# A fused linear attention and ELU feed-forward kernel: the order of the first block's end and the steps in which block 1's units begin

## The chip, the cores and the metric

The kernel runs on one core of one Trainium2 chip. The metric is the device time of one execution in microseconds (us), shown as the median of several runs; the profile is of one further execution. A core has five engines that each work through a queue of their own in order: PE (TensorE, matmuls, with its weight loads shown as PEld), DVE (VectorE), ACT (ScalarE), POOL (GpSimd) and SP (SyncE, which here only issues DMAs). They wait for each other on semaphores.

## The reference

Four batches of 768 tokens with 8 heads of 48 columns go through a linear attention with a decaying state. The result is one row of 384 columns for each of the 3072 tokens, and a two-layer ELU network is applied to it.

```
# attention, for every batch and head
for t in range(S):
    cur = einsum('bhd,bhe->bhde', u * k[t], v[t])
    y[t] = einsum('bhd,bhde->bhe', r[t], state + cur)
    state = w * state + einsum('bhd,bhe->bhde', k[t], v[t])
# x: (3072, 384), w_in: (384, 2048), w_out: (2048, 384)
h = x @ w_in
g = where(h > 0, h, exp(minimum(h, 0)) - 1)
out = g @ w_out
```

## The kernel before

**Blocks, units and slices.** The sequence is cut into 6 blocks of 128 tokens. A block holds 128 tokens of each of the 4 batches; the attention of one batch in one block is a *unit* (n, b). A block's 512 tokens then go through the network in 16 *slices* of 128 hidden columns: the first layer of a slice (`hidden`, L1004, nine matmuls), its ELU, and the second layer (`project`, L1048, nine matmuls). The run is 6 x 16 *steps* (n, f), one slice each. PE takes its large matmuls in pieces of high and low words (`xh`, `xl`, `wh`, `wl`, `gh`, `gl`), so that every layer of a slice has three times three matmuls.

**A unit** turns its r and k by PE (`T`, L606), scales them by powers of the decay (`dr`, `dk`, L666, DVE), multiplies r and k into score matrices (`A`, L740), takes them through a mask (`pa`, `pb`, L821; in block 0 `m0`, `m1`, L666), multiplies with v (`Y`, L779 to L796), and adds to the state (`S` or the end of `Y`, L897, from `krd`, keys scaled on DVE at L712). `ru` and `sum` (L697 to L705) make the token's own term, which ACT and POOL spread into a matrix (`Eq` L810, `Dp` L814). `xh` and `xl` split the result into words.

**A slice's ELU** is a chain over two engines: ACT `neg` (L1013 relu, L1014 exp), DVE `elu` (L1019), ACT `gh` (L1025), DVE `gl` (L1027). **A slice's weights** arrive by DMA (`Lw`, `Lq`) and are split beforehand: ACT `wd` (widen, L549), DVE `ma` (merge, L558), ACT and POOL `sp` (L571, L569), DVE and POOL `r4d`, `r3` (L595, L593).

**The order is written by hand**, and every engine's queue follows it. `START` lists the operations up to the first step: it computes block 0's four units and the first slices' weights. A token is a name and a unit or slice: `Y:3` is the output of unit (0, 3), `S:0` the new state of unit (0, 0), `H:0` the first layer of slice 0 for units 0 and 1 only (256 of 512 columns), `jk:2` two small matmuls that only keep PE busy, `flip` a matmul that makes the table `rev` which `krd` reads, `Ln:1` the loads of unit (1, 1). `ZERO` lists step (0, 0), `FIRST` the other steps of block 0, `LATER` all steps after. In `FIRST` a digit behind a name is a stage of block 1's units, which run inside block 0's steps: unit (1, b) begins in step `BEGIN[b]`, has T and dr/dk in this step (stage 0), A, pa, pb and krd one step later (stage 1), Y two steps later (stage 2) and its new state three steps later (stage 3). `project` of a slice stands one step behind its `hidden`, from step 6 on two steps behind, so step 6 has no `project`.

**PSUM.** Outside the first units, the small results of PE take three banks in turn (tag `rw`): a turned r or k, a score matrix or an added state may be written only when the one three places before in the same bank has been read.

Of the kernel before, what the change touches and what calls it, by code (L numbers as in the profile page):

```python
# [20 lines left out]
B, H, S, D = 4, 8, 768, 48  # L21
# [19 lines left out]
START = """  # L41
Lrk:2 Lv:1 Lrk:3 Lv:2 Lw:0 Lw:2 Lv:3 Lw:1 Lw:4 Lw:3 Lw:5
ub Tr:0 inv ru:0 Tk:0 PT dr:0 dk:0 zw ru:1 Tr:1 dr:1 sum:0 Tk:1 vd:0 A:0 dk:1 ru:2 Tr:2 m0:0 m1:0 Tk:2 A:1 dr:2 dk:2
sum:1 sum:2 vd:1 vd:2 jk:1 Y:0 xh:0 m0:1 m1:1 Tr:3 Tk:3 A:2 xl:0 ru:3 dr:3 dk:3 m0a:2 jk:1 Y:1 m1:2 wd:0 A:3 xh:1 flip
ma:0 sp:0 sum:3 xl:1 wdi:1 rsd:0 Lw:6 vd:3 Y:2 H:0 mai:1 krd:0 spi:1 xh:2 m0:3 m1:3 rsd:2 xl:2 S:0 Ln:0 wdo:1 jk:2 Y:3
H:1 xh:3 xl:3 mao:1 spo:1 krd:1 S:1 Ln:1 wd:2 krd:2 krd:3 rsd:1
"""
ZERO = "Lq hid T0 df0 neg elu gh ma gl rud0 sum0 sp Dp0 r4d r3 wd"
FIRST = """
Lq rk3 v3 Eq1 hid S ns3 A1 T0 rud0 ma sum0 bkA-1 neg df0 elu sp dk0 pa1 brA-1 Y2 gh gl dr0 pb1 r4d xh2 xl2 mbT+1 mrT+1  # L50
proj krd1 swd2 Dp0 r3 rudx rudA-2 sumA-1 wd third tT+0
"""
LATER = """
hid AY tT+0 bkA-1 proj neg elu brA-1 pbA+2 gh gl st nsY+0 xhY+0 xlY+0 paA+1 EqA+1 krA+1 mbT+0 mrT+0 rudA-2
swA+2 sumA-1 rkY+0 vY+0 DpA+0 out
"""
BEGIN = [0, 4, 8, 11]
SCORES = [16, 20, 23, 26] + [13 + 4 * j for j in range(4, 16)]
OUTPUTS = SCORES[1:] + [77]
TURNS = [12] + SCORES[:-1]  # L60
# [3 lines left out]
class Kernel:  # L64
# [307 lines left out]
    def next_loads(self, b):  # L372
        self.raw[1, b] = self.slots[b]
        self.load_rk(1, b)
        self.load_v(1, b)

    def stages(self, n, f):
        return [(f - t, 1, b) for b, t in enumerate(BEGIN) if n == 0 and -1 <= f - t < 4]

    def units_at(self, times, step):  # L380
        return [divmod(2 * B + j, B) for j, t in enumerate(times) if t == step]
# [12 lines left out]
    def step(self, n, f):  # L394
        nc = self.nc

        k = f + 2 if n == 0 else NF + 1
        units = self.stages(n, f)


        last = divmod(n * NF + f - (1 if (n, f) < EARLY else 2), NF)
        both = {
            "ru": lambda n, b: self.current(n, b),
            "kr": lambda n, b: self.key_rest(n, b),
            "A": lambda n, b: self.scores(n, b),
            "sw": lambda n, b: self.decay_state(n, b),
            "rk": lambda n, b: self.load_after(n, b, self.load_rk),
            "ns": lambda n, b: self.new_state(n, b),
            "v": lambda n, b: self.load_after(n, b, self.load_v),
            "sum": lambda n, b: self.current_sum(n, b),  # L410
            "Dp": lambda n, b: self.diag_scores(n, b, 0),
            "Dq": lambda n, b: self.diag_scores(n, b, 1),
            "Ep": lambda n, b: self.diag_scores(n, b, 0, True),
            "Eq": lambda n, b: self.diag_scores(n, b, 1, True),
            "rud": lambda n, b: self.current(n, b, nc.vector),
            "krd": lambda n, b: self.key_rest(n, b, nc.vector),
            "swd": lambda n, b: self.decay_state(n, b, nc.vector),
            "pa": lambda n, b: self.take_scores(n, b, 0),
            "pb": lambda n, b: self.take_scores(n, b, 1),
            "Y": lambda n, b: self.outputs(n, b),  # L420
            "xh": lambda n, b: self.split_x(n, b, 0),
            "xl": lambda n, b: self.split_x(n, b, 1),
        }
        by_pe = {
            "T": lambda n, b: self.turn_in(n, b),
            "dk": lambda n, b: self.decay_k(n, b) if b else None,
            "dr": lambda n, b: self.decay_r(n, b) if b else None,
            "df": lambda n, b: self.decay_in(n, b) if b == 0 else None,
        }
        moved = {  # L430
            "t": lambda n, b: self.turn_blocks(n, b),
            "mb": lambda n, b: self.move_blocks(n, b),
            "mr": lambda n, b: self.gather_blocks(n, b),
            "br": lambda n, b: self.decay_moved(n, b, 0),
            "bk": lambda n, b: self.decay_moved(n, b, 1),
        }
        layer = {
            "hid": lambda: self.hidden(n, f, self.rest_of(n, f)),
            "ma": lambda: self.merge(k),
            "neg": lambda: self.negative(n, f),  # L440
            "sp": lambda: self.split_w(k),
            "r4": lambda: self.rest_w(k, 1),
            "r3": lambda: self.rest_w(k, 0),
            "r4d": lambda: self.rest_w(k, 1, nc.vector),
            "r3d": lambda: self.rest_w(k, 0, nc.vector),
            "elu": lambda: self.elu(n, f),
            "gh": lambda: self.split_g(n, f, 0),
            "gl": lambda: self.split_g(n, f, 1),
            "proj": lambda: self.project(*last) if last in self.g else None,
            "Lq": lambda: [self.load_weights(j) for j in (2 * k + 3, 2 * k + 4)],  # L450
            "wd": lambda: self.widen(k + 1),
            "st": lambda: self.store(last[0]) if last[1] == NF - 1 and last[0] in self.acc else None,
            "out": lambda: self.store_next(),
            "S": lambda: [self.new_state(0, b) for b in (2, 3)] if (n, f) == (0, 1) else None,
            "third": lambda: self.third_slot() if (n, f) == (0, 14) else None,
            "AY": lambda: self.insertion(now),
        }
        now = n * NF + f
        for op in (LATER if n else FIRST if f else ZERO).split():
            if op in layer:  # L460
                layer[op]()
                continue
            if op[-2] in "+-":
                name, times = op[:-3], {"A": SCORES, "Y": OUTPUTS, "T": TURNS}[op[-3]]
                for m, b in self.units_at(times, now - int(op[-2:])):
                    if (name, m, b) not in self.done:
                        self.done.add((name, m, b))
                        {**both, **moved}[name](m, b)
                continue
            name, stage = op[:-1], -1 if op[-1] == "x" else int(op[-1])  # L470
            for at, m, b in units:
                todo = {**both, **by_pe}
                if at == stage and name in todo and (name, m, b) not in self.done:
                    self.done.add((name, m, b))
                    todo[name](m, b)
# [655 lines left out]
```

## Time and profile before

| | |
|---|---|
| median of 3 runs | 511.44 us (510.69 to 511.98) |
| the profiled execution | 509.62 us, of which the span of the trace is 507.9 us |
| PE busy | 493.0 us, 97% of the span |
| DVE, ACT, POOL busy | 304.1, 242.5, 109.6 us |

The span runs from the first to the last instruction of the trace; the profiled execution took 1.7 us more than it. A busy share is the time in which an engine had an instruction running; what an engine costs is read from the waits, since the time of an engine that nobody waits for costs nothing.

### The profile page before, as it was taken

The numbers are of one execution on the slowest core, as the hardware profiler recorded it, in microseconds if no ns is written. First come the engines' busy times: TensorE is split into PE (matmuls) and PEld (weight loads), VectorE is DVE, ScalarE is ACT, GpSimd is POOL, SyncE is SP. The second block draws the span as 40 slices with busy tenths as digits, with TensorE's granted clock in tenths as the row PEclk, the third lists the DMA queues.
The fourth block names the chain that finished last, engine by engine and source line by source line (L and its number), as shares of the span: only waits on it lengthen the run. The fifth ranks groups of instructions, "written<-read, shape, count | busy, mean of one in ns | idle before, by whom it ended". The sixth has DMA issues, their size and how long they took to land.

```text
span 507.9 us, 12144 instructions
## 1 busy us (share of the span) xinstructions
PE 493.0 (97%) x5024; PEld 406.1 (80%) x5024; DVE 304.1 (60%) x528; ACT 242.5 (48%) x462; POOL 109.6 (22%) x145
## 2 busy tenths in 40 slices
PE   7969999999999999999999999999999999999995
PEld 6857887887788888888888888888888878899995
DVE  7786888885865576575574675574664443343331
ACT  2366767744444445435444354354354354344442
POOL 8514334332033141321311212211011000000000
PEclk9998999999999999999999999999999999999999
DMA  8996777765166444625623536316243000011001
GB/s 139 240 184 158 176 187 191 148 130 130 39 140 147 105 71 88 147 66 108 131 49 88 124 59 134 108 36 127 67 96 101 19 0 1 8 27 25 6 0 67
DMA packets 108453, 49.11 MB, mean 97 GB/s; under 512 B 89442, under 2 KB 104292, under 8 KB 108388
## 3 DMA queue, kind: packets, MB, share of 16 engines
q1 hardware_dynamic: 96292, 43.52, 38.5%
q10 hardware_dynamic: 12096, 4.72, 3.9%
q8 instruction: 41, 0.67, 0.6%
q14 instruction: 24, 0.20, 0.1%
HBM read 35.12 MB, written 13.11 MB: 95 GB/s over the span
## 4 chain that ended last, share of the span: by engine, by line
PE 91%; DVE 2%; DMA 2%; ACT 2%; POOL 1%; issue 1%; SPq 0%; DVEq 0%; ACTq 0%
PE ps_acc L1048 40%; PE ps_h L1004 37%; PE ps_y L796 4%; PE ps_a L764 3%; PE ps_a L740 2%; PE ps_y L784 1%; PE ps_y L897 1%; PE ps_y L779 1%; DMA k_t<-in_k_dram 1%; DMA stage<-in_moe_w_in_dram 1%; ACT wide L549 1%; PE ps_y L853 1%; POOL ru L697 0%; PE ps_kT L606 0%; DMA w_col<-in_w_dram 0%
## 5 line engine op out<-in xcount | busy, mean ns | idle before, releaser
L1004 PE MATMUL ps_h<-x,wh 128*128 128x512 f32 (+1 forms) x588 | 180.8, 389 | 0.0
L1048 PE MATMUL ps_acc<-g,wh 128*128 128x512 f32 x480 | 166.3, 401 | 0.0
L1019 DVE SCALAR_TENSOR_TENSOR ps_h<-g,ps_h 128x512 f32<-128x512 f32 x96 | 66.8, 695 | 138.3 <-ACT g L1014 138.1
L1004 PEld LDWEIGHTS ps_h<-x,wh 128*128 128x128 f32 x588 | 109.3, 188 | 23.0 <-issue 0.4
L1013 ACT ACTIVATE g<-ps_h 128x512 f32<-128x512 f32 x96 | 57.5, 598 | 138.5 <-PE ps_h L1004 129.7
L1004 PE MATMUL ps_h<-x,wl 128*128 128x512 f32 (+1 forms) x294 | 114.4, 389 | 0.0
L1048 PEld LDWEIGHTS ps_acc<-g,wh 128*128 128x128 f32 x480 | 90.6, 189 | 22.2 <-issue 0.8
L1048 PE MATMUL ps_acc<-g,wl 128*128 128x512 f32 x240 | 93.8, 391 | 0.0
L1027 DVE SCALAR_TENSOR_TENSOR g<-ps_h,g 128x512 fp32r<-128x512 f32 x96 | 66.4, 691 | 40.8 <-ACT g L1025 36.6
L1025 ACT ACTIVATE g<-ps_h 128x512 fp32r<-128x512 f32 x96 | 57.5, 599 | 67.8 <-DVE ps_h L1019 67.7
L1004 PEld LDWEIGHTS ps_h<-x,wl 128*128 128x128 f32 x294 | 55.2, 188 | 12.7
L1014 ACT ACTIVATE g<-g 128x512 f32<-128x512 f32 x96 | 60.7, 632 | 3.0
L814 POOL TENSOR_TENSOR a<-ident,diag 128x512 f32<-128x512 f32 x20 | 21.2, 1058 | 157.1 <-PE ps_y L897 77.6
L1048 PEld LDWEIGHTS ps_acc<-g,wl 128*128 128x128 f32 x240 | 45.4, 189 | 9.1
L654 POOL TENSOR_TENSOR tb<-rk,qw 128x512 f32<-128x512 f32 x16 | 20.8, 1300 | 67.8 <-DMA rk<-blocks 62.4
L1048 PE MATMUL ps_acc<-wh,g 128*128 128x384 f32 x128 | 35.3, 339 | 0.0
L821 DVE COPY_PREDICATED a<-mask,ps_a 128x512 f32<-128x512 int32 x40 | 29.4, 735 | 0.0
L810 ACT ACTIVATE a<-ident,diag 128x128 f32<-128x128 f32 x80 | 25.3, 390 | 0.7 <-DVE diag L705 0.7
L1048 PEld LDWEIGHTS ps_acc<-wh,g 128*128 128x128 f32 x128 | 23.4, 187 | 1.1 <-issue 0.4
L922 ACT CAST x<-ps_y 128x256 fp32r<-128x256 f32 (+1 forms) x40 | 10.8, 324 | 22.8 <-DVE state L912 21.3
L1048 PE MATMUL ps_acc<-wl,g 128*128 128x384 f32 x64 | 21.6, 337 | 0.0
L569 POOL CAST wh<-stage 128x384 fp32r<-128x384 f32 x16 | 8.9, 554 | 57.1 <-DVE stage L558 57.1
(120 smaller groups left out, 453.9 us busy)
## 6 DMA issues: line engine op xcount, KB each, us to landing
blocks<-tb SPq DMA_DIRECT2D x64, 128.0 KB, 2.3
rk<-blocks SPq DMA_DIRECT2D x16, 512.0 KB, 3.5
stage<-in_moe_w_out_dram SPq DMA_DIRECT2D x16, 383.8 KB, 4.1
stage<-in_moe_w_in_dram SPq DMA_DIRECT2D x64, 95.8 KB, 3.5
out_dram<-stage ACTq DMA_DIRECT2D x80, 48.0 KB, 1.7
r_t<-in_r_dram SPq DMA_DIRECT2D x17, 192.0 KB, 4.6
k_t<-in_k_dram SPq DMA_DIRECT2D x17, 192.0 KB, 5.0
v_t<-in_v_dram SPq DMA_DIRECT2D x17, 192.0 KB, 5.3
```

What stands on the lines that cost most here:

```text
L654: (self.nc.gpsimd if i else self.nc.vector).tensor_mul(dst, src, by)
L796: self.nc.tensor.matmul(y[self.pair(a), t : t + P], lhsT=v[:, d : d + Q], rhs=un["a"][i][:, a, :], start=(n == 0 and j != 1 and len(un["py ...
L810: self.nc.scalar.activation(un["a"][i][:, a, :], self.ident, AF.Copy, scale=diag[:, a : a + 1])
L814: self.nc.gpsimd.tensor_mul(un["a"][i], self.ident.unsqueeze(1).to_broadcast([P, HP, P]), diag.unsqueeze(2).to_broadcast([P, HP, P]),)
L821: self.nc.vector.copy_predicated(un["a"][i], self.mask.bitcast(I32).unsqueeze(1).to_broadcast([P, HP, P]), un["pa"][i].rearrange("p (a t) ...
L1004: self.nc.tensor.matmul(ph[:, part], lhsT=a[:, c * P : (c + 1) * P], rhs=x[:, c, part], start=(c == 0 and i == 0), stop=(c == NC - 1 and i ...
L1013: nc.scalar.activation(g, ph, AF.Relu, scale=-1.0)
L1014: nc.scalar.activation(g, g, AF.Exp, scale=-1.0)
L1019: self.nc.vector.scalar_tensor_tensor(ph, g, -1.0, ph, op0=ALU.add, op1=ALU.max)
L1025: nc.scalar.activation(part, g, AF.Copy, scale=W_SCALE)
L1027: nc.vector.scalar_tensor_tensor(part, g, W_SCALE, self.g[n, f][2].bitcast(F32), op0=ALU.mult, op1=ALU.subtract)
L1048: self.nc.tensor.matmul(at, lhsT=lhs, rhs=rhs, start=(f == 0 and i == 0), stop=(f == NF - 1 and i == 2),)
```

## The change

It edits the four tables and adds one function. In `START`, unit (0, 3)'s masks (`m0:3 m1:3`) and `Y:2`, `Y:3` stand earlier, `flip` stands behind `Y:2`, two keep-warm matmuls become one, and `H:1`, `T` of unit (1, 0), `S:1` and `krd` of units 2 and 3 are gone. In step 0, `T0`, `df0` and the rest of unit (1, 0) are gone, since `BEGIN[0]` is now 2, and `krd` of units (0, 2) and (0, 3) stands in step 0 on DVE. The first layer of slice 1 is done in one piece in step 1. In step 1 the new state of unit (0, 1) and the loads of unit (1, 1) follow `hidden`; in step 2 the new states of units (0, 2) and (0, 3). Block 1's units begin in steps 2, 5, 8, 11 (before 0, 4, 8, 11).

```diff
-sum:1 sum:2 vd:1 vd:2 jk:1 Y:0 xh:0 m0:1 m1:1 Tr:3 Tk:3 A:2 xl:0 ru:3 dr:3 dk:3 m0a:2 jk:1 Y:1 m1:2 wd:0 A:3 xh:1 flip
-ma:0 sp:0 sum:3 xl:1 wdi:1 rsd:0 Lw:6 vd:3 Y:2 H:0 mai:1 krd:0 spi:1 xh:2 m0:3 m1:3 rsd:2 xl:2 S:0 Ln:0 wdo:1 jk:2 Y:3
-H:1 xh:3 xl:3 mao:1 spo:1 krd:1 S:1 Ln:1 wd:2 krd:2 krd:3 rsd:1
+sum:1 sum:2 vd:1 vd:2 jk:1 Y:0 xh:0 m0:1 m1:1 Tr:3 Tk:3 A:2 xl:0 ru:3 dr:3 dk:3 m0a:2 jk:1 Y:1 m1:2 wd:0 A:3 xh:1
+ma:0 sum:3 xl:1 sp:0 wdi:1 vd:3 m0:3 m1:3 Y:2 flip rsd:0 Lw:6 xh:2 xl:2 mai:1 spi:1 krd:0 jk:1 Y:3 H:0 xh:3 xl:3 S:0 Ln:0
+rsd:2 wdo:1 mao:1 spo:1 krd:1 wd:2 rsd:1
-ZERO = "Lq hid T0 df0 neg elu gh ma gl rud0 sum0 sp Dp0 r4d r3 wd"
+ZERO = "Lq hid neg elu kd2 gh gl ma sp kd3 r4d r3 wd"
-Lq rk3 v3 Eq1 hid S ns3 A1 T0 rud0 ma sum0 bkA-1 neg df0 elu sp dk0 pa1 brA-1 Y2 gh gl dr0 pb1 r4d xh2 xl2 mbT+1 mrT+1
+hid S Lq rk3 v3 Eq1 ns3 A1 T0 rud0 ma sum0 bkA-1 neg df0 elu sp dk0 pa1 brA-1 Y2 gh gl dr0 pb1 r4d xh2 xl2 mbT+1 mrT+1
-BEGIN = [0, 4, 8, 11]
+BEGIN = [2, 5, 8, 11]
+    def last_states(self, f):
+        if f == 1:
+            self.new_state(0, 1)
+            self.next_loads(1)
+        elif f == 2:
+            self.new_state(0, 2)
+            self.new_state(0, 3)
-            "S": lambda: [self.new_state(0, b) for b in (2, 3)] if (n, f) == (0, 1) else None,
+            "S": lambda: self.last_states(f) if n == 0 else None,
+            "kd2": lambda: self.key_rest(0, 2, nc.vector),
+            "kd3": lambda: self.key_rest(0, 3, nc.vector),
```

From here on the rows show how the tables change the queues. In the changed kernel the line numbers behind the new function are 8 to 10 higher (L614 becomes L624, L1048 becomes L1058, L914 becomes L924).

The first place on PE is the second layer of slice 0 (`ps_acc`); before, this stood ahead of it, where `ps_h` is the first layer of slice 1, `ps_st` the added states of units (0, 2) and (0, 3) and `ps_a` the scores of unit (1, 0).

```order
L1004 MATMUL ps_h<-x,wl_130 128x256
L897 MATMUL ps_st<-raw 32x48 x32
L740 MATMUL ps_a<-rk 128x128 x8
L1048 MATMUL ps_acc_722<-g_625,wh_129 128x512
L1048 MATMUL ps_acc_722<-g_625,wl_130 128x512
L1048 MATMUL ps_acc_722<-g_628,wh_129 128x512
```

In the changed kernel the same second layer has only one added state ahead of it, that of unit (0, 1), and slice 1's first layer is of 512 columns.

```order
L1014 MATMUL ps_h<-x,wl_130 128x512
L907 MATMUL ps_st<-v_t_73,k_t_72 32x48 x16
L1058 MATMUL ps_acc_638<-g_578,wh_129 128x512
L1058 MATMUL ps_acc_638<-g_578,wl_130 128x512
L1058 MATMUL ps_acc_638<-g_580,wh_129 128x512
```

The states of units (0, 2) and (0, 3) and the scores have left this place; the turn of unit (1, 0), which before stood between the two halves of the first layers just ahead, has left it too.

The second place on PE is the second layer of slice 1 in step 2 of the changed kernel, where `ps_rT` and `ps_kT` are the turned r and k of unit (1, 0).

```order
L1014 MATMUL ps_h<-x,wl_132 128x512
L907 MATMUL ps_st<-raw 32x48 x32
L616 MATMUL ps_rT<-ident,r_t_68 128x128 x4
L616 MATMUL ps_kT<-ident,k_t_69 128x128 x4
L1058 MATMUL ps_acc_638<-g_633,wh_131 128x512
L1058 MATMUL ps_acc_638<-g_633,wl_132 128x512
L1058 MATMUL ps_acc_638<-g_635,wh_131 128x512
```

The states of units (0, 2) and (0, 3) and the turn now stand here, directly behind one another; before, the output `Y` of unit (1, 0) stood at this place.

On ACT the place is from slice 0's `gh` (the first row) on; before, it went on as follows, where `wh` is `sp`, `wide` is `wd`, `a<-ident,diag` is `Eq`, `state` the copy of an added state out of PSUM, and the last two rows are slice 1's relu and exponential.

```order
L1025 ACTIVATE g_625<-ps_h 128x512
L571 ACTIVATE wh_131<-stage 128x384
L549 ACTIVATE wide<-stage 128x768
L810 ACTIVATE a<-ident,diag 128x128 x4
L914 COPY state_61<-ps_st 48x4x48 x2
L914 COPY state_62<-ps_st 48x4x48 x2
L1013 ACTIVATE g<-ps_h 128x512
L1014 ACTIVATE g<-g 128x512
```

In the changed kernel the same `gh` is followed by this, where the sixth to ninth row are slice 1's exponential, `sp`, `gh` and the next `wd`.

```order
L1035 ACTIVATE g_578<-ps_h 128x512
L581 ACTIVATE wh_131<-stage 128x384
L559 ACTIVATE wide<-stage 128x768
L924 COPY state_60<-ps_st 48x4x48 x2
L1023 ACTIVATE g<-ps_h 128x512
L1024 ACTIVATE g<-g 128x512
L581 ACTIVATE wh_133<-stage 128x384
L1035 ACTIVATE g_633<-ps_h 128x512
L559 ACTIVATE wide<-stage 128x768
L924 COPY state_61<-ps_st 48x4x48 x2
L924 COPY state_62<-ps_st 48x4x48 x2
```

The copies of the states of units (0, 2) and (0, 3) stood behind `Eq`, ahead of slice 1's relu; they now stand behind slice 1's `gh` and one more `wd`, and `Eq` has left this stretch for step 3.

On DVE, `ru`, `sum` and `dr`, `dk` of unit (1, 0) move from steps 0 and 1 to step 2, where `dr` and `dk` stand ahead of that step's `elu`. In steps 5 and 8 a unit's last stage and the next unit's first stage now lie in one step, as before only in step 11: DVE's row from a slice's `gl` to the next unit's `dr` is then the same, operation by operation, as in steps 10 and 11 of before.

## Rows read from the trace of the kernel before

**Rows 1.** The page: busy time, share of the span and instructions of PE, PEld, DVE, ACT, POOL.

```profile
PE 493.0 (97%) x5024; PEld 406.1 (80%) x5024; DVE 304.1 (60%) x528; ACT 242.5 (48%) x462; POOL 109.6 (22%) x145
```

**Rows 2.** PE's waits, 0 to 50 us: waiter, releaser: total us, times, longest.

```profile
PE ps_a L740 <- ACT state L914: 4.4, 1, 4.4
...
PE ps_st L897 <- DVE k_t L712: 0.9, 1, 0.9
```

**Rows 3.** PE's waits, 50 us to the end.

```profile
PE ps_a L740 <- DVE rk L666: 1.0, 1, 1.0
```

**Rows 4.** Timeline, 35 to 40 us: start, us, engine, line, operation [idle before <-releaser].

```profile
35.43 1.05 ACT L549 ACTIVATE wide<-stage 128x768 f16<-128x768 bf16 x1
...
38.40 1.30 ACT L914 COPY state<-ps_st 48x192 f32<-48x192 f32 x4
...
39.07 1.78 PE L740 MATMUL ps_a<-rk 48*128 48x128 f32 x14 [4.44 <-ACT state L914]
```

**Rows 5.** Windows, PE alone: stretch, us, busy (count), granted clock, DMA share, GB/s.

```profile
40.00:41.00 1.00, 1.00 (x9) 0.50 0.00 0
...
80.00:82.00 2.00, 0.95 (x12) 1.00 0.15 15
```

**Rows 6.** The chain that ended last, in order of time: start, us, what.

```profile
19.63 1.09 PE ps_a L740 x16
...
21.77 0.79 PE ps_y L853 x24
...
23.44 1.26 PE ps_h L1004 x9
24.70 0.48 PE ps_st L897 x32
25.18 0.64 PE junk L488 x4
...
40.86 3.19 PE ps_acc L1048 x9
...
46.10 0.38 PE ps_y L779 x16
...
48.05 2.27 PE ps_acc L1048 x9
...
52.40 2.06 PE ps_acc L1048 x9
...
56.54 0.44 PE ps_rT L606 x4
```

**Rows 7.** Timeline, 26 to 36 us, ACT and DVE: the operations of a slice.

```profile
26.00 0.65 ACT L549 ACTIVATE wide<-stage 128x384 f16<-128x384 bf16 x1
...
32.08 0.60 ACT L1013 ACTIVATE g<-ps_h 128x512 f32<-128x512 f32 x1
...
32.71 0.63 ACT L1014 ACTIVATE g<-g 128x512 f32<-128x512 f32 x1
...
33.38 0.70 DVE L1019 SCALAR_TENSOR_TENSOR ps_h<-g,ps_h 128x512 f32<-128x512 f32 x1 [0.17 <-ACT g L1014]
...
33.98 0.95 DVE L558 SCALAR_TENSOR_TENSOR stage<-stage,wide 128x768 int32<-128x768 int32 x1
34.11 0.60 ACT L1025 ACTIVATE g<-ps_h 128x512 fp32r<-128x512 f32 x1 [0.76 <-DVE ps_h L1019]
...
34.85 0.68 DVE L1027 SCALAR_TENSOR_TENSOR g<-ps_h,g 128x512 fp32r<-128x512 f32 x1
34.97 0.56 ACT L571 ACTIVATE wh<-stage 128x384 fp32r<-128x384 f32 x1 [0.26 <-DVE stage L558]
```

**Rows 8.** Timeline of DVE, steps 10 to 12: a slice's `gl`, a unit's `dr`, its `krd`.

```profile
89.61 0.69 DVE L1027 SCALAR_TENSOR_TENSOR g<-ps_h,g 128x512 fp32r<-128x512 f32 x1 [0.67 <-ACT g L1025]
...
97.19 0.68 DVE L666 TENSOR_TENSOR rk<-ps_rT,pw 128x512 f32<-128x512 f32 x1
...
102.87 0.55 DVE L712 TENSOR_TENSOR k_t<-k_t,rev 128x384 f32<-128x384 f32 x1
```

## The prediction

> **What bounds the kernel.** The page first: PE is busy for 493.0 of 507.9 us [rows 1], so only PE's time counts, and the other engines only where PE waits. PE's waits come next. Of those that another engine's work ends, three matter: 4.4 us for a copy on ACT, 0.9 us for a DVE multiply ahead of `S:1` [rows 2], and 1.0 us later for `dr` on DVE [rows 3]; the first lies in the steps that the change reorders. The timeline around it shows why. The scores A of unit (1, 0) in step 1 need a bank that still holds an added state; ACT copies it out only at 38.40, since `wd` at 35.43 and `Eq`, which waits for DVE's `ru` and `sum`, stand ahead, and A runs from 39.07 [rows 4]. The windows show a second cost: behind this wait the granted clock is 0.50, the lower level (1.2 GHz), while around the wait of 1.0 us near 80 us it stays at 1.00 [rows 5]. The chain in order of time gives the price: the fourteen matmuls left of A take 1.78 us [rows 4] where a whole A of sixteen takes 1.09, so 0.83 too much, and the second layer behind it takes 3.19 where one takes 2.06, so 1.13 too much [rows 4, 6]. That is 1.96 us.
>
> Nothing ahead of 23.44 us in the trace changes its work, only its order (A:3, flip, `Y:2` become A:3, `Y:2`, flip). I carry the changed queues on from there with the durations of the rows, on that clock.
>
> **What the change removes.** The wait of 4.44 and its clock, 1.96. The wait of 0.9 for `krd:1`: slice 1's first layer now stands ahead of `S:1`. `H:1`'s two halves: 2 x 1.26 against 2.06 for nine full matmuls, 0.46 [rows 6]. One of two keep-warm matmuls, half of 0.64, 0.32 [rows 6]. Sum 8.1 us.
>
> **The new place in step 1.** PE: junk 0.32, `Y:3` 1.67 (23.44 less 21.77), `H:0` 1.26, `S:0` 0.48, so 27.17; the second half 1.26, slice 1 2.06, `S:1` 0.48, so 30.97 [rows 6]. The second layer of slice 0 needs `gh`. ACT starts at 27.17 with the state's copies (half of 1.30), 0.65 for the small `wd`, 1.05 for the next: 29.52 [rows 4, 7]. Relu to the end of `gh` took 2.63 (32.08 to 34.71) [rows 7], so 32.15. PE waits about 1.2, and at its third matmul 0.25 more for `gl` (0.68, ended at 32.9): **1.5 us**. It ends at 34.5.
>
> **The new place in step 2.** ACT's chain to the bank that kT needs: merge 0.95 behind `gl`, `sp` 0.56, `wd` 1.05, unit 1's copies 0.65, slice 1's relu to `gh` 2.63, one more `wd` 1.05, unit 2's copies 0.65 [rows 4, 7]: 32.9 becomes 40.45. PE is there long before: slice 2 2.06, two states 0.96, rT 0.44 [rows 6]: 37.95. **It waits 2.5 us**, in the same manner as before, a bank that ACT frees late.
>
> **Steps 3 to 12.** What is late next is DVE. From 39.5 (slice 1's `gh` ends at 38.75, `gl` takes 0.68) it has a low-word row, `ru` twice and `sum` (0.55 each, as `krd`, which has their size), a merge 0.95, `dr` and `dk` 0.68 each [rows 7, 8], some overlapping by 0.1: `dk` ends near 43.6, ahead of A at 40.5 + 0.44 + 2 x 2.06 = 45.1. Behind it the slice's elu, `gh`, `gl` (1.98), then the stretch from `dr`'s end to `krd`'s end, 5.55 (97.87 to 103.42) [rows 8]: 51.1. Merge, elu, `gh` (2.25) lead to slice 4's `gl` at 53.4; from there to the end of unit (1, 1)'s `dr` is the row of work of steps 10 and 11, 8.26 (89.61 to 97.87) [rows 8]: 61.7. PE reaches A in step 6 after eight slices' layers, A, one `Y` (48.05 less 46.10, 1.95) and a turn [rows 6]: 40.5 + 0.44 + 16.48 + 1.09 + 1.95 + 0.88 = 61.3. It waits 0.4. `krd` follows at 67.25; since step 6 has no second layer, PE is at `Y`'s last part at 66.5 and waits 0.75. By the same rows unit (1, 2)'s `dr` ends at 77.8, with PE there at 76.7 and some 0.1 for each of four changes between kinds of matmul: 0.7. In step 12 PE comes after DVE. Sum 1.85 in place of the 1.0 of before [rows 3]: **0.85 more**. From below the 1.85 is 0 (DVE is ahead); from above it is 1.0 at each of seven meetings (A in 6, 9, 12, `Y` in 4, 7, 10, 13), 7.0. I take the value from the queue, since the stretches of rows 8 are the same work.
>
> **Costed at nothing.** `krd:2` and `krd:3` in step 0 lie in DVE's wait for `gh` and behind the merge, done near 34.4; PE asks for them at 36.6, so 2.2 us of cover. `krd:1` is done near 29.7 and asked for at 30.5; without that cover it would cost what it is late, at most its 0.55. On SP the three loads of unit (1, 1) move behind step 0's five weight loads: the weights come sooner, and the unit needs its loads in step 5, some 20 us later. `Eq` moves to step 3, where ACT lies ahead of A.
>
> **The sum.** 8.1 removed, 1.5 + 2.5 + 0.85 = 4.85 added: 3.3 us less. It lasts to the end, since PE has no other wait behind 50 us [rows 3] and the order behind step 13 is the same. The profiled execution took 509.62, so 506.3; the runs' median is 511.44, and the same difference gives **508.1 us**.
>
> **The rivals.**
>
> *The clock falls in step 2.* The trace has no wait of 2.5 us with its clock: at about 1 us it stays at 1.00, behind 4.44 it is 0.50 [rows 2, 3, 5]. If it falls, the 1.96 is paid again: 510.1. Against it, the new wait is nearer 1 than 4.44 only by little, but two others lie close ahead, with full matmuls between. The Trainium skill ("TensorE: Matmul & The Clock Gate", section on HAM oscillation) says that a PE which waits again and again between short groups of matmuls is throttled again each time and pays the way back each time. By that rule 510.1; the trace agrees for its longest wait alone. Chance 0.13.
>
> *The stall only moves.* Should ACT be 1.9 us later in step 2, kT would wait 4.44 as A did, with its clock: 3.9 more, 512.0. For it speaks that ACT's chain has thirteen links behind each other; against it, that all of them are priced from rows of the same stage. Chance 0.08.
>
> *DVE is overrun* (the other side). Block 1's units now come every three steps from step 2, where the first had four. If each of the seven meetings waits 1.0, the one price that the trace shows, 7.0 replaces 1.85: 513.3. It decides from 3.3 us of extra wait on (no gain), and from 4.8 (clearly slower). Against it: steps 10 to 12 of before hold the same work without a wait. Chance 0.07.
>
> *DVE keeps up.* Where PE comes later than I count, the 1.85 is gone: 506.3. Chance 0.14.
>
> **The numbers.** The forecast has 0.58, its own range 507 to 509.3. About 0.3%, 1.5 us, is what runs of this kernel can tell from no change. Faster by more (under 509.9): 0.56 of the forecast, 0.14, and 0.05 of the clock's case, 0.75. Within: 0.02, 0.08 of the clock's case, 0.06 of the moved stall, and 0.01 of the overrun, 0.17. Slower: 0.02 + 0.06, 0.08. The range of 8 in 10 takes in the clock's case and DVE keeping up: 506.0 to 510.9.
>
> **What would show it.** Right: no wait of A on ACT at 35 us; a wait of kT (L616) on ACT's `state` of about 2.5 us near 38 to 40.5, one of the second layer on `gh` of about 1.2 near 31; clock 1.00 throughout; waits under 1 us at A or `Y` in steps 6, 7 and 9; A of unit (1, 3) in step 12 some 3.3 us earlier than before. Wrong: a clock of 0.50 near 41 us, kT's wait at 4 us or more, or waits on DVE that add up to over 5 us in steps 3 to 13.

## The result and the profile after

The changed kernel took 506.55 us (median of 4 runs, 506.16 to 507.32), the kernel before 511.06 beside it (4 runs, 510.44 to 511.98): a ratio of 0.9912, 95% interval 0.9892 to 0.9932. It is 4.5 us faster; forecast were 3.3 us and 508.1. The profiled execution took 506.66 us, with a span of 504.9.

The page's line of busy time answers to [rows 1]: over the whole run PE is busy 0.3 us longer, and the span is 3.0 us shorter.

```profile
PE 493.3 (98%) x5013; PEld 405.1 (80%) x5013; DVE 303.0 (60%) x528; ACT 241.9 (48%) x462; POOL 109.3 (22%) x145
```

PE's waits up to 50 us, and then those behind 50 us, answer to [rows 2, 3]. The 4.4 us are gone; two waits on ACT and three on DVE stand in the steps that the prediction named.

```profile
PE ps_kT L616 <- ACT state L924: 1.6, 1, 1.6
...
PE ps_acc L1058 <- ACT g L1035: 1.4, 1, 1.4
...
PE ps_a L750 <- DVE rk L676: 0.9, 2, 0.6
PE ps_y L907 <- DVE k_t L722: 0.2, 1, 0.2
```

The timeline gives their places: the second layer of slice 0, the turn of unit (1, 0), A of unit (1, 1), the last part of its `Y`, A of unit (1, 2), and A of unit (1, 3) in step 12, which stood at 98.19 before the change.

```profile
32.66 0.47 PE L1058 MATMUL ps_acc<-g,wh 128*128 128x512 f32 x1 [1.38 <-ACT g L1035]
...
40.31 0.66 PE L616 MATMUL ps_kT<-ident,k_t 128*128 128x128 f32 x4 [1.60 <-ACT state L924]
...
62.22 1.16 PE L750 MATMUL ps_a<-rk 48*128 48x128 f32 x16 [0.36 <-DVE rk L676]
...
67.71 0.55 PE L907 MATMUL ps_y<-v_t,k_t 128*32 128x48 f32 x32 [0.17 <-DVE k_t L722]
...
78.21 1.16 PE L750 MATMUL ps_a<-rk 48*128 48x128 f32 x16 [0.58 <-DVE rk L676]
...
94.98 1.16 PE L750 MATMUL ps_a<-rk 48*128 48x128 f32 x16
```

In the windows the clock behind the new waits is 1.00 (2.4 GHz), where [rows 5] have 0.50 (1.2 GHz).

```profile
40.00:41.00 1.00, 0.69 (x5) 1.00 0.94 206
```

Where the 3.0 us come from shows in the stretch from the first `Y` of block 0 to A of unit (1, 3) in step 12. The first line is before, the second after: length, PE's busy time (matmuls), granted clock.

```profile
13.69:98.19 84.50, 78.13 (x971) 0.98 0.81 185
...
14.09:94.98 80.89, 76.73 (x959) 1.00 0.81 193
```

It is 3.61 us shorter: PE is busy 1.40 us less, and its idle time falls from 6.37 to 4.16. Ahead of it the first `Y` comes 0.40 later, and the time behind it is 0.21 longer, both in parts where PE's work is the same. So the two executions account for 3.0 us. What was open is why the medians lie 4.5 apart.

### The profile page after: what moved, and what is told of

Same layout as the page of the kernel before. It is cut to its first block, busy times and chain, and to the rows that moved or that the text cites. A ratio compares the mean times of both kernels' runs of the same rounds, so it can differ in the third digit from the quotient of the medians.

```text
span 504.9 us, 12122 instructions
## 1 busy us (share of the span) xinstructions
PE 493.3 (98%) x5013; PEld 405.1 (80%) x5013; DVE 303.0 (60%) x528; ACT 241.9 (48%) x462; POOL 109.3 (22%) x145
## 4 chain that ended last, share of the span: by engine, by line
PE 90%; DMA 4%; ACT 2%; DVE 1%; SPq 1%; issue 0%; DVEq 0%; ACTq 0%
PE ps_acc L1058 39%; PE ps_h L1014 37%; PE ps_a L774 4%; PE ps_y L806 3%; DMA stage<-in_moe_w_in_dram 2%; DMA r_t<-in_r_dram 1%; PE ps_y L794 1%; PE ps_a L750 1%; PE ps_y L907 1%; ACT wide L559 1%; PE ps_y L789 1%; PE ps_rT L616 1%; PE ps_kT L616 1%; DMA rev<-in_u_dram 0%; SPq L215 0%
## 5 line engine op out<-in xcount | busy, mean ns | idle before, releaser
L1058 PE MATMUL ps_acc<-g,wh 128*128 128x512 f32 x480 | 165.9, 400 | 1.4 <-ACT g L1035 1.4
L1058 PEld LDWEIGHTS ps_acc<-g,wh 128*128 128x128 f32 x480 | 90.0, 188 | 23.6 <-issue 2.3
L1058 PE MATMUL ps_acc<-g,wl 128*128 128x512 f32 x240 | 93.6, 390 | 0.0
L1058 PEld LDWEIGHTS ps_acc<-g,wl 128*128 128x128 f32 x240 | 45.1, 188 | 9.0
L1058 PE MATMUL ps_acc<-wh,g 128*128 128x384 f32 x128 | 35.2, 338 | 0.0
L1058 PEld LDWEIGHTS ps_acc<-wh,g 128*128 128x128 f32 x128 | 23.4, 187 | 1.1 <-issue 0.4
L1058 PE MATMUL ps_acc<-wl,g 128*128 128x384 f32 x64 | 21.6, 337 | 0.0
```

The source lines that it names most:

```text
L1058: self.nc.tensor.matmul(at, lhsT=lhs, rhs=rhs, start=(f == 0 and i == 0), stop=(f == NF - 1 and i == 2),)
```

## The experiments

Every kernel was timed beside the kernel before on its own chip; in the five groups of runs so timed the median of before was 510.85 to 511.17. "Stretch" is read from each trace: from the first `Y` (first row of `ps_y<-ident,vd`) to A of unit (1, 3) in step 12. It leaves out the first 14 us, which differ from execution to execution.

| kernel | median us (n) | ratio to before, 95% interval | stretch, us |
|---|---|---|---|
| before | 511.06 (4) | 1 | 98.19 - 13.69 = 84.50 |
| before_again | 511.04 (12) | 1.0000, 0.9986 to 1.0014 | 99.78 - 14.59 = 85.19 |
| after | 506.55 (4) | 0.9912, 0.9892 to 0.9932 | 94.98 - 14.09 = 80.89 |
| after_again | 506.87 (6) | 0.9927, 0.9911 to 0.9943 | 95.25 - 14.11 = 81.14 |
| before_begin | 508.23 (7) | 0.9950, 0.9933 to 0.9968 | 97.03 - 14.20 = 82.83 |
| before_begin_s1 | 506.79 (6) | 0.9928, 0.9912 to 0.9944 | 95.03 - 13.70 = 81.33 |
| before_warm | 509.94 (12) | 0.9977, 0.9963 to 0.9991 | 96.58 - 13.63 = 82.95 |
| after_v1 | 507.49 (6) | 0.9926, 0.9907 to 0.9944 | 96.33 - 15.41 = 80.92 |
| after_begin | 507.63 (6) | 0.9944, 0.9929 to 0.9958 | not comparable |
| after_pool | 506.90 (6) | 0.9929, 0.9914 to 0.9943 | 95.05 - 13.98 = 81.07 |
| after_v1pool | 507.80 (6) | 0.9941, 0.9924 to 0.9959 | 95.08 - 13.98 = 81.10 |
| after_df | 509.31 (12) | 0.9969, 0.9956 to 0.9982 | 96.13 - 14.36 = 81.77 |
| after_v4 | 508.92 (8) | 0.9960, 0.9945 to 0.9976 | 97.27 - 15.45 = 81.82 |
| after_less | 505.85 (5) | 0.9883, 0.9865 to 0.9900 | 94.72 - 14.60 = 80.12 |

**before_again**: no edit.

> The kernel before, unchanged, for the clock and the span of each of its runs: its median (511.06) lies 1.4 us above its profiled execution (509.62, mean granted clock 0.996), while the changed kernel's lies on it (506.55, profiled 506.66). Theory: the runs differ in how long the clock stays low behind the wait of 4.44 us, so time and mean clock lie on one line; a mean of 0.996 over 508 us is some 2 us lost, so a run of 511.1 should show about 0.993 (1.4 us more at half speed). Rival: every run shows 0.996 and the 1.4 us lie elsewhere.

Two of its 12 runs had a mean clock of 0.996 and took 509.35 and 509.54; the other ten had 0.990 to 0.993 and took 510.48 to 511.52. Its profiled execution (511.52) shows the difference. The wait is again 4.44, but the windows have the clock at 0.50 still at 43 to 44 us, where the first profile is back at 1.00:

```profile
43.00:44.00 1.00, 1.00 (x4) 0.50 0.90 327
```

In its timeline the rest of A takes 2.07, where [rows 4] have 1.78.

```profile
39.98 2.07 PE L740 MATMUL ps_a<-rk 48*128 48x128 f32 x14 [4.44 <-ACT state L914]
```

Its stretch is 0.69 longer, by the rest of A and the second layer behind it. Another 0.90 lie ahead of it (first `Y` at 14.59 against 13.69). The theory holds for the order of the runs, but the clock behind the wait is only a part of the 1.4 us. The profile on which the forecast stands was one of the cheap executions.

**before_begin**: the start steps alone.

```diff
-BEGIN = [0, 4, 8, 11]
+BEGIN = [2, 5, 8, 11]
```

> The kernel before with the new start steps of block 1's units (2, 5, 8, 11) and nothing else. With no turn in step 0 and no A in step 1, the wait of 4.44 us and the clock's 1.96 go, a wait of some 1.4 us for gh of slice 0 and one of some 0.4 for gh of slice 1 come, and no turn waits for the copies (done near 37.7 by the durations of before, asked for near 38.9). Theory: the gain is that of the start steps alone, the first low words, halves, junk and added states brought nothing that ACT's queue did not take back: time as the changed kernel's, 506.0 to 507.0. Rival: the parts add up as the sum priced them (0.9 for krd:1, 0.46 for the halves, 0.32 for junk are still to be had): 508.2.

The rival was right, to the size. The start steps alone bring 2.7 us in the medians, and 1.7 or 2.4 in the stretch, against the one or the other trace of before. PE's waits still have the 0.9 for `krd:1`; how much is to be had there shows in the next run.

```profile
PE ps_acc L1048 <- ACT g L1025: 1.7, 2, 1.5
...
PE ps_a L740 <- DVE rk L666: 1.2, 2, 0.6
PE ps_st L897 <- DVE k_t L712: 0.9, 1, 0.9
```

**before_begin_s1**: also the added state of unit (0, 1) behind slice 1's first layer.

```diff
-H:1 xh:3 xl:3 mao:1 spo:1 krd:1 S:1 Ln:1 wd:2 krd:2 krd:3 rsd:1
+H:1 xh:3 xl:3 mao:1 spo:1 krd:1 wd:2 krd:2 krd:3 rsd:1
...
+    def last_states(self):
+        self.new_state(0, 1)
+        self.next_loads(1)
+        for b in (2, 3):
+            self.new_state(0, b)
```

> The kernel before with the new start steps, and the added state of unit 1 moved behind slice 1's first layer in step 1, with those of units 2 and 3. The new start steps alone gave 508.2, and PE still waited 0.9 us for krd:1 ahead of it. Theory: the wait goes and slice 0's half, its relu and gh come as much sooner: 0.9 less, 507.3. Rival: the next wait, 1.5 us for gh of slice 0, takes it over, since ACT and DVE pace the first slices: 508.2.

It gained 1.4 us more, or 1.50 in the stretch, over the theory's 0.9. The wait for `krd:1` goes, and ACT is freed as well. In before_begin ACT's copy of this state waits 2.24 us for PE, and the copy and the next `wd` stand ahead of slice 0's relu:

```profile
30.82 0.64 ACT L914 COPY state<-ps_st 48x192 f32<-48x192 f32 x2 [2.24 <-PE ps_st L897]
31.48 1.09 ACT L549 ACTIVATE wide<-stage 128x768 f16<-128x768 bf16 x1
32.59 0.60 ACT L1013 ACTIVATE g<-ps_h 128x512 f32<-128x512 f32 x1
```

Here the relu starts at 29.97, which is 2.12 sooner counted from the first `Y` (16.27 against 18.39), and the second layer waits 0.54 for `gh` in place of 1.49. This kernel has the changed kernel's time (506.79 beside 506.87; stretch 81.33 beside 80.89 and 81.14), although it still does slices 0 and 1 in halves, has both keep-warm matmuls, and keeps the old order of masks, `flip` and added states.

```profile
PE ps_acc L1054 <- ACT g L1031: 1.4, 3, 0.7
PE ps_a L746 <- DVE rk L672: 1.1, 2, 0.6
...
PE ps_y L903 <- DVE k_t L718: 0.3, 2, 0.2
PE ps_y L802 <- ACT g L1019: 0.2, 1, 0.2
```

Its waits in the stretch sum to 3.0 us, the changed kernel's to 4.1 (1.38 + 1.60 + 0.36 + 0.17 + 0.58). PE is busy for 78.15 us of its stretch, in the changed kernel for 76.73. So the rest of the change saves 1.4 us of PE's work, and some 1.1 come back as waiting; the 0.2 to 0.4 that are left in the stretch do not show in the medians.

**before_warm**: 13 keep-warm matmuls in the old wait.

```diff
-Lq rk3 v3 Eq1 hid S ns3 A1 ...
+Lq rk3 v3 Eq1 hid S warm ns3 A1 ...
+"warm": lambda: self.keep_warm(13, "acc2", 1) if (n, f) == (0, 1) else None,
```

> The kernel before with 13 keep-warm matmuls ahead of A of unit (1, 0), in the bank of an accumulator not begun yet: they fill the wait of 4.44 us (13 x 0.32 = 4.2) and do not shorten it, since ACT's copies still end it near 39.7. Theory: the clock's 1.96 us are a cost of their own behind the wait: clock 1.00, A in 1.09 and the second layer in 2.06 us, span 505.9 in place of 507.9; the time 509.1, or 507.7 if the runs of before lose more clock than its profiled execution did. Rival: slow matmuls behind the wait are not the clock's, or these short ones don't hold it: 511.0, no change.

In the profiled execution (507.85 us) the theory is right: clock 1.00, the matmuls took 3.17 us and left 1.31 of the wait, the rest of A took 40.05 - 38.96 = 1.09, and the second layer took 42.24 - 40.05 = 2.19 where it took 3.19 [rows 6]. The stretch is 1.55 shorter, against the 1.96 of the sum, which had set 0.95 for the rest of A and 2.06 for the layer at the full clock.

```profile
34.07 3.17 PE L489 MATMUL junk<-ident 128*128 128x128 f32 x26
...
38.96 1.16 PE L741 MATMUL ps_a<-rk 48*128 48x128 f32 x14 [1.31 <-ACT state L915]
...
40.00:41.00 1.00, 1.00 (x6) 1.00 0.00 0
```

The median fell by only 1.0 us, and the runs' mean clocks do not say why. Seven of the twelve are at 0.994 or below and have a median of 510.19, but the four at 0.998 or more took 509.03 to 510.02, and the profiled one, at 0.997, was the fastest. A mean below 1.000 need not cost time: this one is lost from 503 us on, behind PE's last matmul at 500.15.

```profile
504.00:505.00 1.00, 0.00 (x0) 0.50 0.11 27
```

Whether the matmuls hold the clock in every execution, and what else sets the runs' times, stays open.

**after_v1**: both waits on ACT shortened.

```diff
-rsd:2 wdo:1 mao:1 spo:1 krd:1 wd:2 rsd:1
+rsd:2 wdo:1 mao:1 spo:1 krd:1 rsd:1
-ZERO = "Lq hid neg elu kd2 gh gl ma sp kd3 r4d r3 wd"
+ZERO = "Lq hid neg elu kd2 gh gl w2 ma sp kd3 r4d r3 wd"
-hid S Lq rk3 v3 Eq1 ns3 A1 T0 rud0 ...
+hid S Lq rk3 v3 Eq1 ns3 A1 p2 T0 rud0 ...
+"w2": lambda: self.widen(2),
+"p2": lambda: self.project(*last) if (n, f) == (0, 2) else None,
```

> The changed kernel with its two PE waits on ACT shortened: wd of slice 2 behind gh of slice 0 (proj of slice 0 starts 1.05 us sooner, wait 1.4 to some 0.4), and in step 2 the second layer of slice 1 ahead of the turn (PE waits some 0.8 for gh in place of 1.6 for the bank). The turn of unit (1, 0) ends some 1.9 us sooner. First theory: the waits are PE's alone, 1.9 us less to the end, 504.7. Rival: DVE's queue from slice 1's gl on gains only 0.7 us, so A of unit (1, 1) in step 6 waits 1.5 in place of 0.36, and 0.7 us are left: 505.9.

Neither size came. Counted from the first `Y`, A of unit (1, 0) comes 0.66 sooner (45.72 - 15.41 = 30.31, the changed kernel 45.06 - 14.09 = 30.97); A of unit (1, 1) comes at 48.18 against 48.13. The gain is gone, the stretch is the same (80.92), and the time, 507.49, is no shorter than the changed kernel's. DVE shows why: its merge in step 2 starts at 42.35 - 15.41 = 26.94, in the changed kernel at 40.98 - 14.09 = 26.89. PE ran ahead of an engine that was no earlier.

```profile
42.35 0.95 DVE L570 SCALAR_TENSOR_TENSOR stage<-stage,wide 128x768 int32<-128x768 int32 x1
...
63.59 1.16 PE L752 MATMUL ps_a<-rk 48*128 48x128 f32 x16 [0.55 <-DVE rk L678]
```

**after_again**: no edit.

> The changed kernel, unchanged, beside the kernel before on the same chip, for the clock and span of its runs. The kernel before, run again, showed 509.4 us where the mean clock was 0.996 and 510.5 to 511.5 where it was 0.990 to 0.993, and its second profile has the clock at 0.50 for 2.9 us longer behind the wait of 4.44. Theory: the changed kernel has no such stretch, so its runs lie closer together and their clock near 1.00 (0.996 to 1.00), median 506.5. Rival: the median of before was of that chip, and here the two differ by the traces' 3.0 us: 508.

506.87, with clocks of 0.997 to 1.000. The distance to before is 4.0 us here; in the stretch it is 85.19 - 81.14 = 4.05 between the two second profiles and 84.50 - 80.89 = 3.61 between the first ones.

**after_begin**: `BEGIN = [2, 6, 9, 12]`.

> The changed kernel with block 1's units begun in steps 2, 6, 9 and 12 in place of 2, 5, 8 and 11. Theory of the prediction: DVE falls behind because units come every three steps, so one more step for the first takes the first wait of A for dr away (0.36 us) and shortens the later ones: 506.0. Rival: the wait for dr is made within its own step (the multiply stands behind elu, merge and low words in DVE's queue, and the kernel before waited 1.05 us with four steps between units): waits of the same size, 506.5.

Both wrong: 0.8 us slower. One wait of 1.86 for `dr` stands in step 7 in place of three on DVE that sum to 1.11. (A of unit (1, 3) stands in step 13 here, so the stretch does not compare.) The order of the steps gives a reason, which no run took apart: step 6 has no second layer, so PE reaches step 7's A that much sooner, while DVE's work for the unit is the same.

```profile
66.58 1.16 PE L750 MATMUL ps_a<-rk 48*128 48x128 f32 x16 [1.86 <-DVE rk L676]
```

**after_pool**: the products r*u*k of block 1's units on POOL.

```diff
-... A1 T0 rud0 ma sum0 ...  swd2 Dp0 r3 rudx ...
+... A1 T0 ru0 ma sum0 ...  swd2 Dp0 r3 rux ...
```

> The changed kernel with the two multiplies r*u*k of block 1's four units on POOL (about 1.0 us each there, 0.56 on DVE), where POOL is idle. DVE has 1.1 us less ahead of each unit's dr. Theory: DVE's queue is what the PE waits of 0.36, 0.17 and 0.58 us in steps 6, 7 and 9 hang on, so they go: 1.1 us less, 505.4. Rival: dr waits behind elu and gl, which ACT times, and not behind the multiplies: under 0.3 us, 506.3.

No change (506.90). The multiplies left DVE, but the rows of DVE that overlap them on POOL were drawn out, here for unit (1, 1). The first two rows of the timeline are DVE's in this kernel, the other two the multiplies on POOL.

```profile
54.59 1.23 DVE L605 SCALAR_TENSOR_TENSOR wl<-stage,wh 128x384 fp32r<-128x384 f32 x1
...
56.27 1.02 DVE L732 TENSOR_TENSOR sw<-state,pw 48x192 f32<-48x192 f32 x2
...
54.37 1.03 POOL L707 TENSOR_TENSOR ru<-r_t,u_b 128x384 f32<-128x384 f32 x1
55.48 1.21 POOL L708 TENSOR_TENSOR ru<-ru,k_t 128x384 f32<-128x384 f32 x1
```

In after_again DVE's same two rows are these:

```profile
54.71 0.55 DVE L605 SCALAR_TENSOR_TENSOR wl<-stage,wh 128x384 fp32r<-128x384 f32 x1
...
55.71 0.71 DVE L732 TENSOR_TENSOR sw<-state,pw 48x192 f32<-48x192 f32 x2
```

(1.23 - 0.55) + (1.02 - 0.71) = 0.99 of the 1.12 us were lost. The Trainium skill ("SBUF — State Buffer", section "Who interferes with whom") says that a DVE instruction with two SBUF inputs contends with a GpSimd instruction that reads SBUF, for ports that one of them locks; the rows agree, in that DVE's took longer beside POOL's. So this run says nothing of the theory: DVE was not relieved.

**after_v1pool**: both edits.

> Both: the second layer of slice 1 ahead of the turn and wd of slice 2 behind gh of slice 0 (which alone made A of unit (1, 0) 0.66 us earlier, counted from the first Y, and gave it back by step 6, where DVE was not earlier), with the multiplies on POOL. Theory: with DVE's queue relieved the 0.66 us stay, and the waits of 1.1 go as well: 504.8. Rival: steps 0 to 6 are paced by the exchange between ACT and DVE for each slice (relu, exp, elu, gh, gl, merge), which neither edit shortens: 506.3.

507.80, stretch 81.10: no gain either. Of the two, the rival's size is nearer, but its cause isn't shown, since DVE was not relieved here either.

**after_df**: `dr` and `dk` together ahead of `elu`.

```diff
-"dk": lambda n, b: self.decay_k(n, b) if b else None,
-"dr": lambda n, b: self.decay_r(n, b) if b else None,
-"df": lambda n, b: self.decay_in(n, b) if b == 0 else None,
+"dk": lambda n, b: None,
+"dr": lambda n, b: None,
+"df": lambda n, b: self.decay_in(n, b),
```

> The changed kernel with one edit in DVE's order: for units (1, 1) to (1, 3) the two decay multiplies dr and dk stand together ahead of the slice's elu, as they do for unit (1, 0); before, dk stood behind elu and dr behind gl. dr ends 1.4 us sooner (elu and gl, 0.69 each, are behind it now), which is more than the waits of A for it in steps 6 and 9 (0.36 to 0.57 and 0.6). Theory: the place of dr in DVE's queue makes the two waits, not DVE's load: 0.9 to 1.2 us less, 505.8. Rival: DVE is full there, and elu, 1.3 us later, gives the time back at a second layer or at Y's last part: 506.9, no change.

Slower by 2.4 us. The waits of A for `dr` are gone, so their place was read rightly; but DVE now takes the scores through the mask later, and `Y` waits for a bank of them:

```profile
PE ps_y L789 <- DVE a L831: 1.0, 1, 1.0
PE ps_y L907 <- issue: 0.5, 1, 0.5
PE ps_y L907 <- DVE k_t L722: 0.5, 3, 0.2
PE ps_y L806 <- ACT g L1023: 0.2, 1, 0.2
```

The stretch accounts for 0.6 to 0.9 of the 2.4; 0.5 is the second line, a wait in block 1 (185 us); the rest is not explained.

**after_v4**: after_df and after_v1, with slice 1's ELU begun a step earlier.

```diff
-ZERO = "Lq hid neg elu kd2 gh gl ma sp kd3 r4d r3 wd"
+ZERO = "hid neg h1 elu rs1 Lq kd2 gh gl w2 n1 ma e1 sp g1 kd3 r4d l1 r3 wd"
```

> The changed kernel with dr and dk ahead of elu, and with the exchange between ACT and DVE for slice 1 (relu, exp, elu, gh, gl) begun as soon as its first layer is there, in a gap of ACT of 1.6 us ahead of the copy of slice 2's weights; also wd of slice 2 behind gh of slice 0, slice 1's low words behind slice 0's elu, and slice 1's second layer ahead of the turn. By the rows of the changed kernel slice 1's gh ends near 36 in place of 38.7, so the waits of 1.4 and 1.6 us shrink to some 1.0 in all and the 1.1 of steps 6 to 9 go. Theory (ACT and DVE, slice by slice, pace the start; PE follows): 3 us less, 503.9. Rival: what PE gains is taken back by DVE's queue up to step 6, as when only PE's order was changed: 505.8.

508.92, 2 us slower: both theories missed. DVE, asked for slice 1's `elu` earlier, delivers slice 2's low words later (the multiply at L613 starts 21.50 after the first `Y`, in the changed kernel at 20.64), and after_df's wait is there as well.

```profile
PE ps_h L1022 <- DVE wl L613: 1.3, 1, 1.3
PE ps_y L797 <- DVE a L839: 1.2, 1, 1.2
```

**after_less**: two multiplies fewer on DVE for each of block 1's units.

```diff
-"rud": lambda n, b: self.current(n, b, nc.vector),
+"rud": lambda n, b: self.no_current(n, b) if n == 1 else self.current(n, b, nc.vector),
+    def no_current(self, n, b):
+        self.units.setdefault((n, b), {})["ru"] = self.raw[n, b][0][:, :, 0:D]
```

> The changed kernel without the products r*u*k of block 1's four units: DVE leaves out two multiplies of 0.56 us for each, and sums r in their place, so those units' diagonals are not the reference's. Nothing is put on POOL, so no instruction of DVE is drawn out (with the multiplies on POOL one low-word row took 1.23 in place of 0.55 and one state row 1.02 in place of 0.71, which ate 0.99 of the 1.12 us). Theory: DVE's load from a slice's gl to dr paces steps 3 to 9, so the waits of 0.36, 0.17 and 0.58 us go and 0.9 to 1.1 us are gained: 505.9 beside the 506.87 of the changed kernel. Rival: ACT's exchange with DVE for each slice paces them, and the multiplies stood in its gaps: under 0.3 us, 506.7.

The theory is right: 505.85, 1.0 less than after_again (5.3 under the kernel before on its chip, where the changed kernel lies 4.0 to 4.5 under it), and the stretch is 0.77 to 1.02 shorter. Both waits for `dr` are gone, and the waits on ACT are unchanged:

```profile
PE ps_kT L619 <- ACT state L927: 1.6, 1, 1.6
...
PE ps_acc L1061 <- ACT g L1038: 1.4, 1, 1.4
PE ps_y L910 <- DVE k_t L725: 0.2, 1, 0.2
```

## Why the prediction was right, and what it missed

**The wait and its clock.** Right: neither is in the changed kernel's trace. The rival of the falling clock did not happen (1.00 behind 1.38 and behind 1.60). What the clock does behind the 2.5 that were forecast no run shows, since no such wait came. The price of 1.96 was not the clock's alone: at the full clock behind a shorter wait, before_warm's A and layer take 0.27 us more than the sum had set for them, and its stretch is 1.55 shorter than that of before. And it was read from a cheap execution: before_again's stretch is 0.69 longer for the same wait.

**The wait for `krd:1`, 0.9.** Right that it goes, too small: moving that state alone was worth 1.4, since ACT's copy of it no longer holds up slice 0's relu and `gh`.

**The halves and the keep-warm matmul, 0.46 + 0.32.** This step failed: not as PE's time, but as a gain. A kernel that still has the halves and both keep-warm matmuls has the same time (before_begin_s1); what PE saves it waits for ACT and DVE. Which part of the rest of the change the waits take back, no run took apart.

**The wait of the second layer, 1.5.** `gh` ended as forecast (18.43 after the first `Y`, forecast 18.46). PE waits 1.38 for it, and the layer took 35.02 - 32.66 = 2.36, 0.30 over 2.06: 1.7.

**The wait of kT, 2.5.** 1.60, by the mechanism named. Counted from the first `Y`, the bank came free at 26.22, forecast at 40.45 - 13.69 = 26.76, and PE was there at 24.62 in place of 24.26.

**DVE's meetings, 1.85.** 1.11 (1.33 in after_again), by the mechanism named: from the start of slice 4's `gl` (53.82) to the end of unit (1, 1)'s `dr` (61.40 + 0.68) it is 8.26, the figure that the queue was carried on with.

```profile
53.82 0.69 DVE L1037 SCALAR_TENSOR_TENSOR g<-ps_h,g 128x512 fp32r<-128x512 f32 x1 [0.67 <-ACT g L1035]
...
61.40 0.68 DVE L676 TENSOR_TENSOR rk<-ps_rT,pw 128x512 f32<-128x512 f32 x1
```

after_less shows that it is DVE's load, after_df that putting `dr` and `dk` ahead of `elu` does not better it. "DVE keeps up" is what after_less buys: 505.85. "DVE is overrun" and "the stall only moves" did not happen.

**The sum.** A in step 12 comes 94.98 against 98.19, 3.2 us sooner, and 3.6 counted from the first `Y` (forecast 3.3). That it comes so near is luck in part. The forecast took 2.7 us off PE's busy time (1.96 + 0.46 + 0.32) and only 0.5 off its waits (4.4 + 0.9 + 1.0 gone, 1.5 + 2.5 + 1.85 new); measured are 1.4 and 2.2.

The step that set the number wrong is the last: "the same difference gives 508.1". The changed kernel took 506.55 us, 1.6 less. Of these, 0.4 is the kernel before: 511.44 was the median of the three runs ahead of the forecast, 511.06 the one beside the changed kernel. The other 1.2 is that the medians lie 4.5 apart and not 3.3. The profiled execution of before lay 1.4 us under its median, the changed kernel's lies on its own (506.66 beside 506.55), so the profiles' difference is not that of the medians. Half of the 1.4, 0.7, is the longer low clock, if before_again's execution, the only other one of before with a trace, stands for typical runs (its mean clock is 0.993, that of most 0.990 to 0.993); the change takes it away with its wait. Of the other half, some can be the start, below, and some is not accounted for.

## What to carry to other kernels

Where two engines hand work back and forth, ask of each saving whether the engine that is waited for gets earlier too: here one table of start steps and one moved state bring 4.1 us, and all the rest of the change nothing that the medians show. A price for a lowered clock that is read from one execution is one draw; a mean clock over the run is no substitute, since it also counts the time behind the last matmul, so look at the stretch behind the wait in more than one trace. In after_df and after_v4, taking a wait away by moving work up DVE's queue moved the wait to what stood behind it.

## What the runs showed of the hardware

The start of the kernel runs faster or slower, from execution to execution. The first turn of r took 0.65 us in the timeline of the first profile of before:

```profile
6.00 0.65 PE L606 MATMUL ps_rT<-ident,r_t 128*128 128x128 f32 x4
```

In the second one it took 1.11, and the turn of k behind it 1.06. The windows' column of the clock shows 1.00 there in both, so that these turns ran at the lower level is not shown:

```profile
6.70 1.11 PE L606 MATMUL ps_rT<-ident,r_t 128*128 128x128 f32 x4
7.60 1.06 PE L606 MATMUL ps_kT<-ident,k_t 128*128 128x128 f32 x4
```

The first `Y` stood between 13.63 and 15.45 us in the fourteen traces, whatever the kernel, so 1 us of a difference between two single traces can be the start's alone. That the same kernel comes to full speed at different points in different runs is also what the Trainium skill says ("TensorE: Matmul & The Clock Gate", section "What's actually happening"); by their durations at the start the two profiles of before agree, by their column of the clock they do not.
